# Spectral mixing beside softmax attention: tokens folded four ways instead of two, and the symmetry checks made on chip

## The chip, the core and the metric

One core of a Trainium2 chip runs the whole program. The metric is the device time of one execution in microseconds (us). Its engines are TensorE (PE: matmuls, PEld: its weight loads), VectorE (DVE), ScalarE (ACT), GpSimd (POOL) and SyncE (SP, which here issues all DMAs of the main path).

## The reference

Two branches work on separate inputs, and their outputs stand side by side in `out` (2048 tokens, 2 x 448 features).

```python
# A: Fourier mixing, S = 2048, D = 448
a = einsum("bsd,ed->bse", x, dft_hid_re);  b = einsum("bsd,ed->bse", x, dft_hid_im)
y = einsum("ts,bse->bte", dft_seq_re, a) - einsum("ts,bse->bte", dft_seq_im, b)
# B: softmax attention, 16 heads of 28
q, k, v = split(x @ wqkv);  p = softmax(q @ k.T * 28 ** -0.5);  out = (p @ v) @ wo
```

The DFT matrices are inputs of 2048 x 2048 and 448 x 448. The kernel may use their symmetry only where it finds that the given matrices have it.

## The kernel before

Matmuls run in f32r with each operand split into a high and a low part, so that a product takes three matmuls (high-high, high-low, low-high). The value product of attention is plain f32 and takes two passes.

**Attention.** For each head, 16 key tiles of 128 by 4 query chunks of 512. `first_tiles` makes the scores of the first key tile, which give the row shift: the score matmul (L1107), an ACT copy (L1111), DVE transposes and reductions (L1112, L1113, L1119, L1124), a DVE transpose back (L1133), a cast of the shift into row 96 of q (L1136, POOL or DVE), an addition (L1138, DVE or POOL) and an exponential (L1140). A bank of a first tile is free only after the ACT copy and the DVE transpose. `scores` then has 60 score matmuls a head (L1166), each with an exponential on ACT (L1172); `sums` has the value matmuls in bursts of two key tiles (L1149); `out_of` closes a head (L1198 to L1215). Six of the eight PSUM banks are used for scores and the values' sum, two for everything else. The output projection (L1328) stands behind the last head.

**Fills.** Everything else on PE is put between the scores: the seven q/k projections (L736, L772), the values, and the spectral branch. A planner, `Schedule`, plays the program through once with a table of durations and writes the instructions out, engine by engine, in the order in which it saw them start. Each task has a key; an engine takes the lowest key of those that are ready. `fkey` spreads the keys of the fills over the time up to `T_FILL` in proportion to their planned matmul time, `F_TOTAL`. On the chip each engine, and SP's queue of DMAs, keeps that order.

**Spectral branch.** `hidden` (L888) makes, for the cosine and then the sine part, 8 token tiles of u: tokens s and 2048 - s are added or subtracted (`Pair`, L868), and a tile is multiplied by 226 of the 448 feature columns (`load_folded`, L550); the other columns follow from symmetry at the end. `sequence` (L960) multiplies 8 output tiles by u: for each of two halves it loads a piece of the sequence matrix, splits it (`Piece`, L574: POOL cast L458, POOL subtraction L591) and does 9 matmuls of 452 or 226 columns (L994). The mirrored images of that matrix have to be compared with it before its symmetry may be used. For that, DMAs first write turned copies of both matrices into HBM (`turn_rows`, L854, tensors `wr`); `sequence` reads them back, and `mirrored` (L651) takes differences on POOL or DVE (L654, L672) and their largest values on DVE (L645). The cosine part's result goes through HBM (`y_d`). At the end `flag` puts all checks together; where one fails, general loops (`any_scores`, `any_sequence`) do the work again.

The lines that set the order around the change:

```python
T_ATT, T_END, T_FILL, T_OUT = 56.0, 670.0, 735.0, 690.0
fill_s, bank_s = Slots(banks[:NFILL]), Slots(banks[NFILL:])    # NFILL = 2
M512, M448, M225, MS = 0.2335, 0.2050, 0.1900, 0.2365          # planned us of a matmul
at = 6 + IN + V_PACE * (HEAD - IN)
return at + (f - HEAD) * (T_FILL - at) / (F_TOTAL - HEAD)      # fkey, behind the values
either = {"POOL": 1.2, "DVE": 0.83}                            # planned us of a difference
```

## Time and profile before

| | us |
|---|---|
| runs (median; lowest to highest) | 771.15; 768.4 to 773.13 |
| the profiled execution, first to last instruction | 771.8 |
| PE busy / ACT / DVE / POOL in it | 748.9 / 609.4 / 521.2 / 362.2 |
| end of head 0's values, of head 15's (copies L1198) | 122.0, 733.2 |

The profile comes from one execution, whose span is 0.65 us above the median of the runs; no other time is listed for it. Busy times of PE include the part of a matmul that overlaps the next one.

### The profile page before, as it was taken

Reading aid. Unit: us, or ns where it says so; the run is one execution under the profiler, and the core shown is the slowest. Engines: PE = TensorE matmul, PEld = TensorE weight load, DVE = VectorE, ACT = ScalarE, POOL = GpSimd, SP = SyncE. Lnnn points to the kernel's source line nnn. Section 1 sums busy time; section 2 is a strip of 40 time slices with the busy share of each in tenths; the row PEclk is TensorE's granted clock in tenths of the full one; section 3 lists DMA queues with packets and bytes.
Section 4 is the critical chain, followed back from the end, with each engine's and each line's share of the span. In section 5 each row is a group of like instructions: output and inputs, shape, how many; then the busy total and the mean of one; then the engine's idle time right before and its main releaser. Section 6 shows DMA issues by size and latency. Waiting matters only on the chain.

```text
span 771.8 us, 13016 instructions
## 1 busy us (share of the span) xinstructions
PE 748.9 (97%) x4150; PEld 425.8 (55%) x4150; DVE 521.2 (68%) x962; ACT 609.4 (79%) x1231; POOL 362.2 (47%) x448
## 2 busy tenths in 40 slices
PE   9999999999999999899899999999999989999997
PEld 7899655555555555445455554534545435434596
DVE  5547813656364948899896959695999779834371
ACT  6403888999898988979788989886989869898842
POOL 7211500223032646677674817374787658343510
PEclk9999999999999999999899999999999989999999
DMA  8866845376415635674537657554576585516153
GB/s 309 272 233 186 252 125 159 123 193 199 134 61 146 200 105 164 182 224 135 159 116 221 207 151 230 154 184 131 166 231 215 150 238 158 148 54 209 52 188 137
DMA packets 113603, 133.16 MB, mean 173 GB/s; under 512 B 50345, under 2 KB 63208, under 8 KB 113528
## 3 DMA queue, kind: packets, MB, share of 16 engines
q1 hardware_dynamic: 113528, 132.26, 57.0%
q8 instruction: 35, 0.57, 0.3%
q14 instruction: 40, 0.33, 0.1%
HBM read 101.17 MB, written 49.19 MB: 195 GB/s over the span
## 4 chain that ended last, share of the span: by engine, by line
PE 72%; DVE 9%; DMA 6%; POOL 4%; ACT 4%; issue 3%; SPq 1%; POOLq 0%; ACTq 0%; DVEq 0%
PE bank L1166 24%; PE bank L1149 23%; PE bank L736 12%; PE bank L1328 5%; PE bank L994 4%; ACT kept L1172 3%; PE bank L772 2%; PE bank L908 2%; DMA wraw<-wim 2%; PE bank L1107 1%; DMA wr<-wim 1%; DMA wraw<-wr 1%; DVE kept L1138 1%; DVE mb L1133 1%; DVE mb L1112 1%
## 5 line engine op out<-in xcount | busy, mean ns | idle before, releaser
L1172 ACT ACTIVATE kept<-bank 128x512 f32<-128x512 f32 x960 | 487.0, 657 | 77.6 <-PE bank L1166 77.3
L1166 PE MATMUL bank<-q,k 98*128 98x512 f32 x960 | 341.7, 428 | 6.6 <-ACT kept L1172 4.1
L1166 PEld LDWEIGHTS bank<-q,k 98*128 98x128 f32 x960 | 173.9, 189 | 176.3 <-issue 95.0
L1149 PE MATMUL bank<-kept,v 128*32 128x512 f32 x2048 | 247.8, 608 | 0.0
L1149 PEld LDWEIGHTS bank<-kept,v 128*32 128x32 f32 x2048 | 55.7, 110 | 120.9 <-issue 117.9
L1136 POOL CAST q<-mb 1x512 fp32r<-1x512 f32 x39 | 32.2, 842 | 79.4 <-DVE mb L1133 60.7
L1112 DVE STREAM_TRANSPOSE mb<-bank 128x512 f32<-128x512 f32 x64 | 45.1, 707 | 24.0 <-PE bank L1107 21.9
L1111 ACT ACTIVATE kept<-bank 128x512 f32<-128x512 f32 x64 | 38.4, 651 | 26.0 <-PE bank L1107 21.1
L1209 POOL TENSOR_TENSOR kept<-kept 128x512 f32<-128x512 f32 x16 | 20.7, 1291 | 80.4 <-DVE kept L1204 58.5
L645 DVE TENSOR_REDUCE far<-wraw 128x1 f32<-128x508 f32 (+1 forms) x90 | 57.3, 665 | 0.9 <-POOL wraw L654 0.4
L736 PE MATMUL bank<-big,whi 128*128 128x512 f32 x154 | 57.4, 397 | 0.3 <-DVE wd L753 0.3
L994 PE MATMUL bank<-big,whi 128*128 128x452 f32 x128 | 48.2, 376 | 5.2 <-POOL whi L458 5.2
L591 POOL TENSOR_TENSOR wlo<-wraw,whi 128x512 fp32r<-128x512 f32 (+1 forms) x33 | 43.5, 1319 | 7.9 <-ACT whi L585 5.2
L654 POOL TENSOR_TENSOR wraw<-wraw,wraw 128x508 f32<-128x508 f32 x33 | 37.9, 1149 | 15.2 <-DMA wraw<-wr 6.0
L1140 ACT ACTIVATE kept<-kept 128x512 f32<-128x512 f32 x64 | 41.2, 720 | 4.4 <-DVE kept L1138 3.7
L1133 DVE STREAM_TRANSPOSE mb<-am 128x512 f32<-128x512 f32 x64 | 43.3, 697 | 1.5 <-POOL q L1136 0.5
L1113 DVE TENSOR_REDUCE qm<-mb 128x16 f32<-128x512 f32 x64 | 43.0, 675 | 1.1
L1138 DVE TENSOR_TENSOR kept<-kept,mb 128x512 f32<-128x512 f32 x40 | 38.8, 986 | 0.2
L458 POOL CAST whi<-wraw 128x512 fp32r<-128x512 f32 x30 | 20.0, 665 | 37.1 <-DMA wraw<-wre 13.9
L736 PE MATMUL bank<-wd,big 128*128 128x448 f32 x176 | 37.0, 364 | 0.0
L1200 DVE STREAM_TRANSPOSE kept<-kept 128x512 f32<-128x512 f32 x16 | 11.2, 700 | 37.8 <-ACT kept L1198 37.8
L753 DVE TENSOR_TENSOR kept<-bank,kept 128x512 fp32r<-128x512 f32 x20 | 13.3, 687 | 34.3 <-ACT kept L752 34.2
(165 smaller groups left out, 1017.2 us busy)
## 6 DMA issues: line engine op xcount, KB each, us to landing
wraw<-wr SPq DMA_DIRECT2D x60, 256.0 KB
qkd<-kept SPq DMA_DIRECT2D x40, 256.0 KB
wraw<-xa SPq DMA_DIRECT2D x32, 256.0 KB
wraw<-wre SPq DMA_DIRECT2D x32, 256.0 KB
wr<-wre SPq DMA_DIRECT2D x31, 256.0 KB
wr<-wim SPq DMA_DIRECT2D x31, 256.0 KB
k<-qkd SPq DMA_DIRECT2D x64, 112.0 KB
q<-qkd SPq DMA_DIRECT2D x64, 112.0 KB
```

The source lines that it names most:

```text
L591: b = sch.add(e, at, lambda g: eng[g].tensor_tensor(self.lo.t[:, :n], raw.t[:, :n], f32(self.hi.t)[:, :n], op=ALU.subtract), deps=[a], acq ...
L645: far_done.append(dve(key, lambda: nc.vector.tensor_reduce(far[:, part, n:n + 1], t(), axis=AX.XY, op=ALU.max, apply_absolute_value=True), ...
L736: nc.tensor.matmul(o.t[:, :cols], w(), x(), start=(i == 0), stop=(i == n - 1))
L994: nc.tensor.matmul(o.t[:, :2 * E if slot and slot.pool is whi else E], a, b, start=first, stop=final)
L1112: t = dve(key, lambda o=o, tm=tm: nc.vector.transpose(tm.t, o.t), 0.73, deps=[m], acq=[tm], use=[o], lock=[o], own=RAW_S)
L1113: rs.append(dve(key, lambda tm=tm, c=c: nc.vector.tensor_reduce(qm.t[:, 0, c * NT:(c + 1) * NT], tm.t.rearrange("p (j r) -> p j r", r=32), ...
L1133: t = dve(key, lambda mb=mb, c=c: nc.vector.transpose(mb.t, f32(am.t)[:, c * NT:(c + 1) * NT].unsqueeze(2).to_broadcast([P, NT, 32])), 0.7 ...
L1138: sh = sch.add({"DVE": 0.92, "POOL": POOL_2}, key, lambda e, s=s, mb=mb: eng[e].tensor_tensor(s.t, s.t, mb.t, op=ALU.add), deps=[t, made[c ...
L1140: shown.append(act(key, lambda s=s: nc.scalar.activation(s.t, s.t, AF.Exp, scale=SCALE), ACT_S, deps=[sh], use=[s.pair]))
L1149: nc.tensor.matmul(o.t[c * VW:(c + 1) * VW, :], VT[h].t[:, kt // 4, kt % 4, :], tiles[c].t, start=(kt == 0), stop=(kt == NT - 1))
L1166: m = pe(key, lambda e, o=o, q=q, kt=kt: nc.tensor.matmul(o.t, KT[h][kt // 4].t[:KM, kt % 4 * P:(kt % 4 + 1) * P], q.t[:KM, :], start=True ...
L1172: es[h, kt].append(act(key - 20, lambda o=o, p=p: nc.scalar.activation(p.t, o.t, AF.Exp, scale=SCALE), deps=[m], use=[o, p.pair]))
```

## The change

The spectral branch is written anew.

- **Tokens** s, 2048 - s, 1024 - s and 1024 + s are added and subtracted at once (`tokens`), so that even and odd rows of the sequence matrix, taken apart, need a quarter of it. Features d and 448 - d are folded as well. `features` multiplies the folded tokens (8 fills of 12 matmuls of 226 columns), `sequence` the result (8 fills of 12 or 13).
- Of the sequence matrices only a **base** of 512 x 512 entries each is split and kept on chip (`convert`). All results stay on chip between the two parts.
- The other entries are **compared** with the base in eight `check`s, which only load rows (`Rows`, `Turned`), take differences of up to 1024 columns (L944, POOL or DVE) and their largest values (L887, DVE). The checks' keys are 75, 141, 207 and so on up to 537. No turned copy is written to HBM.
- The planner's durations: 0.107 for a matmul of 226 columns, and 2.3 (POOL) or 1.2 (DVE) for a difference of 1024 columns. `F_TOTAL` is smaller; `T_FILL` and the attention's keys are as before.

The core of the diff:

```diff
-    M512, M448, M225, MS = 0.2335, 0.2050, 0.1900, 0.2365
+    M512, M448, M226, MS = 0.2335, 0.2050, 0.1070, 0.2365
-    F_TOTAL = 7 * F_QKV + F_V + 2 * (NH + 1) * (4 * M448 + 3 * M225) + 2 * NH * (8 * M448 + 9 * M225)
+    F_TOTAL = 7 * F_QKV + F_V + (8 * 12 + 2 * 6 + 8 * 12 + 4 + 2 * 6 + 1) * M226
-    either = {"POOL": 1.2, "DVE": 0.83}
+    either = {"POOL": 2.3, "DVE": 1.2}
+    half_e = {"POOL": 1.25, "DVE": 0.65}
-    wr_d = [dram.tile([NT, P, NH, P], F32, name=f"wr{i}") for i in range(2)]
-    wraw = new("wraw", [P, 4, P], F32, 8, True)
+    raw_s = new("raw", [P, 2, CH], F32, NRAW, True)
...
+    def tokens(c, key, after):
...
+        ts = sch.add(either, key + 1, lambda g: eng[g].tensor_tensor(a.t, n.t, r.t, op=ALU.add), deps=[*ln, *z], use=[n, a, r])
+        td = sch.add(either, key + 1, lambda g: eng[g].tensor_tensor(r.t, n.t, r.t, op=ALU.subtract), deps=[ts], use=[n, r])
...
+    def features(i, ready):
+        for q in range(4):
+            key, o = fkey(12, M226), fill_s.slot()
...
+            end = fill(jobs, key, o, [*x_ready[i], *ready])
...
+    def largest(t, ready, part, key, use, rows=P, d=1.2, n=None):
...
+        far_done.append(dve(key, lambda: nc.vector.tensor_reduce(
+            far[:rows, part, n:n + 1], t(), axis=AX.X, op=ALU.max, apply_absolute_value=True), d, deps=[*ready, far_clear], use=use))
...
+    def check(part, ps, i, key, step):
...
+        def against(x, y, op, at, cols, of=None, deps=()):
+            of = of or cols
+            d = {"POOL": 2.3, "DVE": 1.2} if cols == slice(0, H1) else {"POOL": 1.25, "DVE": 0.65}
+            return sch.add(d, at, lambda g: eng[g].tensor_tensor(x.t[:, cols], x.t[:, cols], y.t[:, of], op=op),
+                           deps=[*x.ld, *y.ld, *deps], use=[x.raw, y.raw])
+
+        def natural(r, at):
+            a, b = Rows(part, r, ps, i, 0, at), Rows(part, r, ps, i, 1, at + 0.4)
+            x = against(b, a, turn, at + 4, slice(0, H1))
+            largest(lambda: b.t, [x], part, at + 5, [b.raw])
+            return a, against(a, a, up, at + 5, high, back, [x])
...
+    def convert(part, n, key, after):
+        r = Rows(part, 0, ps, i, 0, key, 5)
...
-    made = hidden(0, w_first, load_folded(w_first, 0, key - 10, after=[v_last[0], *staged]), x_users)
...
-    sequence(1, made, range(NH - 1), free=[NH - 2])
+    for i in range(2):
+        for c in (2 * i, 2 * i + 1):
+            tokens(c, fkey(0, 0) - 30 + 3 * (c % 2), x_users)
+        features(i, wd_ready)
+    peak = middle(wd_ready)
+    fx_last = last[0]
+    for part in range(2):
+        for n in range(4):
+            convert(part, n, fkey(0, 0) - 18 + 2 * n, [last[0]])
+        special(part, fkey(0, 0) - 14, [fx_last])
+        sequence(part, peak)
+    for n in range(8):
+        check(n // 4, n // 2 % 2, n % 2, CHECK_AT + n * CHECK_STEP, CHECK_STEP / 4)
...
-    sequence(1, made, [NH - 1], True)
```

What that does to the order is shown at three places. In the changed kernel scores are L1221, value matmuls L1204, projections L687 and spectral matmuls L855. First PE in head 0, between two bursts of values, before: eight scores with four projection matmuls (L736) between them.

```order
L1166 MATMUL bank_146<-q_108,k_105 128x512
L1166 MATMUL bank_142<-q_109,k_105 128x512
L1166 MATMUL bank_141<-q_110,k_105 128x512
L1166 MATMUL bank_143<-q_111,k_105 128x512
L1166 MATMUL bank_145<-q_108,k_102 128x512
L736 MATMUL bank_140<-big,whi 128x512
L1166 MATMUL bank_146<-q_109,k_102 128x512
L736 MATMUL bank_140<-big,wlo 128x512
L1166 MATMUL bank_142<-q_110,k_102 128x512
```

And the same group in the changed kernel, up to its burst of values.

```order
L1221 MATMUL bank_126<-q_89,k_86 128x512
L1221 MATMUL bank_123<-q_90,k_86 128x512
L1221 MATMUL bank_122<-q_91,k_86 128x512
L1221 MATMUL bank_125<-q_92,k_86 128x512
L1221 MATMUL bank_127<-q_89,k_83 128x512
L1221 MATMUL bank_126<-q_90,k_83 128x512
L1221 MATMUL bank_123<-q_91,k_83 128x512
L1221 MATMUL bank_122<-q_92,k_83 128x512
L1204 MATMUL bank_124<-kept_107,v_87 32x512 x2
```

The group has no fill any more; four groups in head 0 are of this form. Over the heads 1 to 15 the fills on PE stand like this (counted from the order, up to the last value matmul of each head):

| head | 1 | 2 | 3 | 4 | 5 | 6 | 7 | 8 | 9 | 10 | 11 | 12 | 13 | 14 | 15 |
|---|---|---|---|---|---|---|---|---|---|---|---|---|---|---|---|
| before, 512 columns | 38 | 36 | 34 | | | | | | | | | | | | |
| before, 452 and 448 | | | 1 | 26 | 16 | 23 | 23 | 21 | 16 | 11 | 15 | 18 | 17 | 6 | 17 |
| before, 226 | | | 1 | 20 | 14 | 17 | 20 | 23 | 17 | 14 | 16 | 20 | 20 | 7 | 9 |
| change, 512 columns | 34 | 11 | 36 | 36 | 15 | | | | | | | | | | |
| change, 448 | | | | | | | | | | | | | | | 9 |
| change, 226 | | | | | | | 48 | 8 | 52 | 46 | 56 | 11 | | | |

Second, PE in head 7 of the changed kernel, where the first spectral matmuls stand (`big` is the folded tokens here, `wd` the folded features).

```order
L1221 MATMUL bank_124<-q_95,k_83 128x512
L855 MATMUL bank_121<-wd,big 128x226
L1221 MATMUL bank_125<-q_96,k_83 128x512
L855 MATMUL bank_121<-wd,big 128x226 x3
L1221 MATMUL bank_122<-q_93,k_83 128x512
L855 MATMUL bank_121<-wd,big 128x226 x2
```

In the old kernel such places hold one spectral matmul of 452 or 226 columns after a score; now one to three of 226. Third, DVE between the first tiles of heads 2 and 3, before. (L1200 to L1207 close a head, `wraw` holds raw tokens or matrix pieces, L753 splits a projection.)

```order
L1207 TENSOR_REDUCE ok<-sm_135 128x1
L877 TENSOR_TENSOR wraw_79<-wraw_81,wraw_79 128x4x127
L879 TENSOR_TENSOR wraw_79<-xraw,wraw_79 128x4
L1077 TENSOR_REDUCE ok<-v_107 128x1
L753 TENSOR_TENSOR kept_125<-bank_140,kept_125 128x512
L1112 STREAM_TRANSPOSE mb_133<-bank_146 128x512
L1113 TENSOR_REDUCE qm_136<-mb_133 128x16
```

And there in the changed kernel (L944 and L887 belong to a check, L704 is the old L753).

```order
L944 TENSOR_TENSOR raw_75<-raw_75,raw_73 128x1024
L887 TENSOR_REDUCE far<-raw_72 128x1
L887 TENSOR_REDUCE far<-raw_75 128x1
L887 TENSOR_REDUCE far<-raw_73 128x1
L944 TENSOR_TENSOR raw_71<-raw_71,raw_70 128x1024
L704 TENSOR_TENSOR wd<-bank_121,wd 128x512
L887 TENSOR_REDUCE far<-raw_71 128x1
L887 TENSOR_REDUCE far<-raw_70 128x1
L887 TENSOR_REDUCE far<-raw_74 128x1
L944 TENSOR_TENSOR raw_72<-raw_72,raw_74 128x1024
L704 TENSOR_TENSOR wd<-bank_120,wd 128x512
```

Between the first tiles of these two heads DVE now has 12 reductions and 3 differences of 1024 columns of a check, where a few operations on tokens stood.

682 lines of the change are left out of this document (342 added, 340 removed).

## The prediction

> **What bounds the kernel now.** I read the page's busy times and its chain first, then single stretches by time, because the shares of a whole span mix stages with different limits.
>
> ```profile
> span 771.8 us, 13016 instructions
> PE 748.9 (97%) x4150; PEld 425.8 (55%) x4150; DVE 521.2 (68%) x962; ACT 609.4 (79%) x1231; POOL 362.2 (47%) x448
> ...
> PE 72%; DVE 9%; DMA 6%; POOL 4%; ACT 4%; issue 3%; SPq 1%; POOLq 0%; ACTq 0%; DVEq 0%
> ```
>
> PE looks like the only limit: busy for 97% of the span and 72% of the chain that ended last. If that were all, each matmul removed would shorten the run by its own time. The attention loop says otherwise. One of its groups is two key tiles: 8 score matmuls (L1166) into the 5 banks left to scores, 8 exponentials (L1172), and a burst of value matmuls (L1149). The view by stretches, cut at the starts of four value bursts, gives length, then busy time of PE, PEld, DVE, ACT, POOL, and the granted clock:
>
> ```profile
> 100.60:105.45 4.85, 4.85 (x33) 2.61 (x35) 0.69 (x1) 4.03 (x10) 0.00 (x0) 1.00 0.61 178
> 680.06:685.00 4.94, 4.69 (x25) 1.83 (x24) 3.13 (x4) 4.94 (x12) 4.28 (x4) 1.00 0.14 47
> 685.00:689.93 4.93, 4.68 (x25) 1.84 (x25) 0.00 (x0) 4.93 (x12) 0.00 (x0) 1.00 0.13 37
> 689.93:694.43 4.50, 4.50 (x25) 1.84 (x25) 0.00 (x0) 4.03 (x10) 0.00 (x0) 1.00 0.00 0
> ```
>
> The first group also carries projection matmuls put between the scores ("fills"); the other three carry none. Without fills a group still takes 4.50 us, and 4.93 when ACT has two first-tile activations beside its 8 exponentials (ACT is then busy from end to end). So a group gains at most 0.35 us from losing all its fills: ACT and the way through the banks hold the rest, and PE's 97% is largely filler. The pace per head is in the chain, where 32 value matmuls together mark the end of one head and the start of the next:
>
> ```profile
> 120.03 3.57 PE bank L1149 x32
> 160.24 3.57 PE bank L1149 x32
> 199.79 3.57 PE bank L1149 x32
> ...
> 360.04 3.57 PE bank L1149 x32
> 406.43 3.57 PE bank L1149 x32
> 445.84 3.57 PE bank L1149 x32
> 484.99 3.57 PE bank L1149 x32
> 529.59 3.57 PE bank L1149 x32
> ...
> 656.15 3.57 PE bank L1149 x32
> 694.50 3.57 PE bank L1149 x32
> 702.68 1.91 PE bank L1149 x15
> ...
> 731.19 1.85 PE bank L1149 x16
> ```
>
> Heads 1 to 14 run from 120.03 to 694.50, 574.5 us. Quiet heads take 39.15 to 39.6 us (445.84 to 484.99; 160.24 to 199.79). The head before 694.50, with only 13 fills, takes 38.35. Heads 7 and 10 take 46.39 and 44.60, and the bad ones look like this:
>
> ```profile
> 342.00:386.00 44.00, 41.53 (x223) 21.94 (x225) 39.66 (x73) 36.51 (x75) 31.23 (x42) 0.92 0.47 141
> 428.00:466.00 38.00, 38.00 (x227) 19.38 (x225) 27.58 (x52) 33.69 (x69) 16.78 (x20) 1.00 0.63 177
> 507.00:552.00 45.00, 41.79 (x225) 20.37 (x225) 34.31 (x54) 34.87 (x70) 29.35 (x33) 0.92 0.52 151
> 590.00:637.00 47.00, 41.57 (x224) 19.83 (x222) 37.19 (x64) 36.05 (x72) 31.54 (x36) 0.93 0.63 188
> ```
>
> Each bad stretch has more DVE and POOL work than the quiet one, PE idle for 2.5 to 5.4 us, and a mean clock of 0.92 or 0.93. At 39.4 for thirteen heads and 38.35 for the lightest, heads 1 to 14 would take 550.6, so **stalls cost 23.9 us** of the 574.5.
>
> **The change, step by step.** The sum is against the profiled 771.8 us (first to last instruction), 0.65 above the median of the runs, 771.15.
>
> *Fills.* What one costs PE is its distance to the next start:
>
> ```profile
> 188.17 0.39 PE L736 MATMUL bank<-big,whi 128*128 128x512 f32 x1
> 188.40 0.39 PE L1166 MATMUL bank<-q,k 98*128 98x512 f32 x1
> ...
> 615.66 0.27 PE L994 MATMUL bank<-big,wlo 128*128 128x226 f32 x1
> 615.77 0.40 PE L1166 MATMUL bank<-q,k 98*128 98x512 f32 x1
> 616.01 0.37 PE L994 MATMUL bank<-big,whi 128*128 128x452 f32 x1
> 616.22 0.42 PE L1166 MATMUL bank<-q,k 98*128 98x512 f32 x1
> ...
> L994 PE MATMUL bank<-big,whi 128*128 128x452 f32 x128 | 48.2, 376 | 5.2 <-POOL whi L458 5.2
> ...
> L994 PE MATMUL bank<-big,wlo 128*128 128x226 f32 x128 | 34.8, 272 | 1.4 <-POOL wlo L591 1.3
> ```
>
> That is 0.23 us for 512 columns, 0.21 for 452 and 0.11 for 226 (the groups' 376 and 272 ns include what overlaps the next one). With its smaller groups the old spectral branch has 200 of 452 and 198 of 226, 63.8 us; the new one has 221 of 226, 24 us. These 40 us are not the gain, since a fill stands mostly where PE waits for a bank. What counts is how many heads become light. Per head 1 to 14 the order now gives 34, 11, 36, 36, 15 wide fills, none, then 48, 8, 52, 46, 56, 11 narrow ones, none, none. I price heads 1, 3, 4 at 39.5, heads 9 to 11 (5 to 6 us of fills) at 39.1, heads 2, 5, 7 at 38.6, and 6, 8, 12, 13, 14 at 37.8: 38.35 less two or three of the 0.25 to 0.35 us that fills cost a group. Sum 540.6 against 550.6: **-10.0**. Bounds: +0 if every head kept 39.4, and -20 if a light head came down to 37.1.
>
> *Head 0.* Of 200 projection matmuls before its end 176 are left. Eight go from the start, where PE feeds itself (1.9 us); sixteen go from four groups (4 x 0.35): **-3.3**, at most 24 x 0.23 = 5.6, at least 0 if a load is late instead.
>
> *Head 15* runs from 702.68 to 731.19 in six groups of 4.75 on average; its 17 spectral fills go, and 4.50 each gives **-1.5**. The output projection behind it is the same work: 0.
>
> *The old stalls.* They go with their causes, for instance PE waiting for a converted piece at L458:
>
> ```profile
> 624.68 0.47 PE L994 MATMUL bank<-big,whi 128*128 128x452 f32 x1 [2.37 <-POOL whi L458]
> ```
>
> The turned copies in HBM, the loads behind them and the 16 column tiles of each half go, so **-23.9**, from 0 to -23.9.
>
> *The new stalls.* What is late next is DVE. It makes each head's first tiles, and a first tile's bank stays taken until DVE has transposed it, so a DVE that lags holds up scores at once.
>
> ```profile
> L1112 DVE STREAM_TRANSPOSE mb<-bank 128x512 f32<-128x512 f32 x64 | 45.1, 707 | 24.0 <-PE bank L1107 21.9 <-ACT kept L1111 1.8
> ...
> L645 DVE TENSOR_REDUCE far<-wraw 128x1 f32<-128x508 f32 x60 | 38.8, 662 | 0.8 <-POOL wraw L654 0.4
> L1138 DVE TENSOR_TENSOR kept<-kept,mb 128x512 f32<-128x512 f32 x40 | 38.8, 986 | 0.2
> ...
> L654 POOL TENSOR_TENSOR wraw<-wraw,wraw 128x508 f32<-128x508 f32 x33 | 37.9, 1149 | 15.2 <-DMA wraw<-wr 6.0 <-DMA wraw<-wre 5.5 <-DMA wraw<-wim 3.2
> ...
> L753 DVE TENSOR_TENSOR kept<-bank,kept 128x512 fp32r<-128x512 f32 x20 | 13.3, 687 | 34.3 <-ACT kept L752 34.2
> ```
>
> The new checks use operations of 1024 columns, which no row shows. A reduction of 1024 is bounded by one and by two of 508, 0.66 and 1.32; I take 1.25, near two, as the length is in the columns. A two-operand operation of 1024 is bounded by 0.69 below and 2 x 0.99 above; I take 1.7, near two of L1138, whose operands lie in SBUF as well. Between the first tiles of heads 2 and 3 the new order has 12 reductions (11.4 us), 3 operations of 1024 (5.1), three smaller (2.5) and 4 of L704 (4 x 0.69). The head's own chain is about 16 (the quiet 27.6 of 38 us above, less what I count there as spectral work, an estimate). Sum 37.7 of a 39.5 us head, where before some 25 stood. The same count gives 30 to 35 for most of heads 4 to 11, about 39 around head 8 where tokens are folded, and 16 from head 13 on. Old heads with 34 to 40 us of DVE work lost 5 to 7 us, clock included. I expect two such heads, at 6 each, and 2 us where the first matmul of a fill batch waits for its conversion: **+14**. Bounds: 0, and 24 as before; beyond that lies a rival.
>
> The Trainium skill ("VectorE: DVE Perf Modes", the section on the TRN2 errata) gives (N+151)/0.96 for such an fp32 operation, 1.22 us as an estimate at 1024; for 512 it gives 0.69, as L753 shows and L1138 does not. By it the 19 wide operations on DVE take 9 us less, and the sum would be some 3 us lower.
>
> *SP and DMA.* SP keeps its length, 717 rows for 720, and the copies into HBM go, while loads now come in 512-byte runs. A late q or k load would hold up scores; I take 0, from -2 to +6 (one wait like the DMA ones above).
>
> Sum: 771.8 - 10.0 - 3.3 - 1.5 - 23.9 + 14 = **747**.
>
> **The rivals.**
> *No stall is left* (0 for +14): 733. For it: five late heads have hardly any fills and little DVE work. Against it: DVE at 37 to 39 us in two places. If light heads also reach 37.1, 724.
> *Stalls as before* (24 for 14): 757, to 766 with the q and k loads late as well. For it: 1024-column operations on POOL would be twice 1.15, and what waits for one waits longer.
> *Slower: DVE takes over the pace.* If in each of the eight heads with a check a wide operation took 3.3 us (two of L1138 and a POOL operation to wait for) and the small ones 1.7, DVE would need 44.5 us where the head has 39.5, and PE would idle and be clocked down as in the 0.92 rows: 8 x 6 on 733 is 781. It decides from 42 us of DVE per head on. The old 39.66 of 44 speaks for it, L645 (662 ns, beside busy POOL as well) against.
> *Slower: PE is clocked down in light heads.* A group has 3.7 us of PE work (1.85 value, 8 x 0.23 scores); at half clock 7.5 instead of 4.5, over 35 groups, +105: about 840. The three fill-free groups above at clock 1.00 speak against it. The Trainium skill ("TensorE: Matmul & The Clock Gate", on psum-queue depth-cycling) says that short idles between groups of matmuls that cycle through banks can make the clock fall and rise; by that rule this rival is the forecast, and the trace disagrees with 1.00.
> *The change doesn't do what it says*: if the flag at the end found the folded matrices unequal, the general loops would run behind everything, 512 more matmuls of 448 columns and their loads, far over 1000.
>
> **How the numbers follow.** Forecast (738 to 757) 0.54; no stall (724 to 738) 0.16; stalls as before (757 to 766) 0.20; DVE 0.06; clock 0.03; fallback 0.01. A measurement of this kernel can tell about 1% from no change: 763.4 to 778.9 is "same". Of the stalls-as-before case 0.08 lies there and 0.01 of the DVE case, so faster 0.82, same 0.09, slower 0.09. The range 730 to 766 leaves out half of the no-stall case and the last three, 0.18.
>
> **What would show it.** Starts of 32 value matmuls 37.5 to 38.5 apart in heads 12 to 14, fill-free groups of 4.5 at clock 1.00, ACT busy for over 90% there, PE's share below 97%. Right on the stalls: PE idle and a clock under 1.00 in heads 2, 3 and around 8, none behind head 12. I am wrong if light heads stay at 39.4 (something else than PE and ACT paces a head), if wide DVE operations take over 2.5 us, or if q or k loads head SP's waits.

## The result: 14% slower, 882 us

The changed kernel takes 882.1 us (median of four runs, 880.4 to 883.8), where the kernel before takes 769.8 beside it (four runs): a ratio of 1.144, 95% interval 1.139 to 1.149. The forecast was 747, range 730 to 766, and none of its slower rivals (781, 840, over 1000) is near either. The experiments below find why: many of the new loads and stores are shaped so that only about 2 of the 16 DMA engines carry each of them, and the q, k and v loads of attention stand behind them on the same queue.

The page of the changed kernel, its first lines and the chain that ended last:

```profile
span 882.2 us, 12611 instructions
PE 780.7 (88%) x3971; PEld 406.7 (46%) x3971; DVE 492.1 (56%) x826; ACT 613.9 (70%) x1225; POOL 318.0 (36%) x314
...
PE 49%; DMA 17%; DVE 10%; SPq 10%; ACT 5%; issue 4%; POOL 3%; POOLq 0%; DVEq 0%; ACTq 0%
```

No compute engine has more instructions than before, and DVE and POOL are busy for less time (492 for 521 us, 318 for 362). PE shows 32 us more, though with 179 matmuls fewer; its clock fell in the long heads, as shown below. What has grown in the chain is DMA, from 6% to 17%, and SP's queue, from 1% to 10%. The chain in order of time gives the heads (start of 32 value matmuls, length):

```profile
178.24 5.35 PE bank L1204 x32
223.62 3.57 PE bank L1204 x32
273.67 3.57 PE bank L1204 x32
...
635.21 3.57 PE bank L1204 x32
674.67 3.57 PE bank L1204 x32
728.20 3.57 PE bank L1204 x32
766.18 3.57 PE bank L1204 x32
804.16 3.57 PE bank L1204 x32
...
774.36 1.85 PE bank L1204 x16
778.87 1.85 PE bank L1204 x16
```

The light heads came out as forecast: 37.98 us from 728.20 to 766.18 and again to 804.16 (37.8 was the estimate), with a group of 4.51 from 774.36 to 778.87. Most of the heads with comparisons, tokens and output stores take 44 to 62 us instead: 45.38 and 50.05 in the first three rows, 53.53 from 674.67 to 728.20. The chain is dense with waits for loads there. The waits of DVE and POOL, in total, times and longest:

```profile
POOL raw L944 <- DMA raw<-wre: 60.7, 11, 17.0
DVE ok L1132 <- DMA v<-vd: 47.2, 12, 8.8
DVE raw L944 <- DMA raw<-wre: 30.8, 10, 8.3
DVE raw L807 <- POOL raw L806: 26.6, 3, 10.9
```

Operands of the comparisons (L944), tokens (L807 behind L806) and v (L1132) all arrive late. SP's 904 issues of loads and stores take 577 us, where the 767 of before take 410. (With SP's rows for semaphores that is 597 and 449, the figures in the first expectation below.) The stretch in which one comparison's turned loads end (SP's rows, then the view of the DMA engines from 458 to 462; its first row is their mean busy share in tenths, in 40 slices) shows how:

```profile
453.66 1.27 SPq L904 DMA_DIRECT2D raw<-wim  x2
455.03 5.81 SPq L924 DMA_DIRECT2D raw<-wim  x5
460.94 1.39 SPq L1101 DMA_DIRECT2D k<-qkd  x1
...
DMA  1111111111111111111111111111111111111111
GB/s 46 41 41 41 51 41 41 41 41 51 41 41 41 51 41 41 41 51 41 41 41 51 41 41 41 41 51 41 41 41 51 41 41 41 51 41 41 41 51 41
DMA packets 345, 0.17 MB, mean 43 GB/s; under 512 B 6, under 2 KB 345, under 8 KB 345
q1 hardware_dynamic: 345, 0.17, 14.4%
```

Five turned loads (64 KB each, the fifth a single column) hold SP for 5.81 us. Behind them, for 4 us, 43 GB/s move: 345 packets, or 86 per us, at 14.4% of 16 engines, which is **2.3 engines**. Just before, from 455 to 457, with the last two loads of rows under way and the first turned loads just issued, the same view has these rows:

```profile
DMA packets 929, 0.47 MB, mean 233 GB/s; under 512 B 19, under 2 KB 929, under 8 KB 929
q1 hardware_dynamic: 929, 0.47, 97.2%
```

Pieces of the same 512 B run at 465 per us there, on 15.6 engines. Small pieces are not what is slow. Nor is it their place in memory: a busy engine moves 37 pieces of the turned loads per us and 30 of the rows (86 / 2.3 and 465 / 15.6). The other engines have nothing to do.

Two more records of this trace bear that out. Each load updates a semaphore, a counter on which later instructions wait, as its parts land: 16 times for every load of rows (L904), but only 3 times for each of the 80 turned loads (L924), the 36 turned loads of tokens and weights (L567) and the eight stores of L1065. And the five turned loads above are issued in 0.59, 0.55, 1.54, 1.50 and 1.44 us; the first four land at 459.44, 460.94, 462.45 and 463.94, so 1.5 us apart. From the third on an issue takes as long as one such load takes to land behind the one before it, and the k load can be issued only at 460.94. Counted from the start of their issue, q and k loads land after 2.92 and 3.73 us on average, against 2.49 and 2.78 in the kernel `floor` of experiment 12. So they lose about a microsecond or less behind their issue; the rest of their delay lies ahead of it, where SP is held: in the head from 372.3 to 428.4 it is issuing for 49.7 of the 56.1 us.

### The profile page after: what moved, and what is told of

Read it like the earlier page. It is cut to its first block, busy times and chain, and to the rows that moved or that the text cites. A ratio compares the mean times of both kernels' runs of the same rounds, so it can differ in the third digit from the quotient of the medians.

```text
span 882.2 us, 12611 instructions
## 1 busy us (share of the span) xinstructions
PE 780.7 (88%) x3971; PEld 406.7 (46%) x3971; DVE 492.1 (56%) x826; ACT 613.9 (70%) x1225; POOL 318.0 (36%) x314
## 4 chain that ended last, share of the span: by engine, by line
PE 49%; DMA 17%; DVE 10%; SPq 10%; ACT 5%; issue 4%; POOL 3%; POOLq 0%; DVEq 0%; ACTq 0%
PE bank L1221 18%; PE bank L1204 15%; PE bank L687 8%; ACT kept L1227 4%; PE bank L1377 4%; DMA raw<-wre 4%; DMA raw<-wim 3%; DMA v<-vd 2%; DMA raw<-xa 2%; PE bank L855 2%; SPq L924 2%; PE bank L723 2%; DMA raw<-wd 2%; SPq L904 1%; DVE far L887 1%
## 5 line engine op out<-in xcount | busy, mean ns | idle before, releaser
L1221 PE MATMUL bank<-q,k 98*128 98x512 f32 x960 | 363.3, 455 | 73.0 <-ACT kept L1166 30.9
L1221 PEld LDWEIGHTS bank<-q,k 98*128 98x128 f32 x960 | 181.5, 197 | 278.4 <-issue 103.2
L1204 PE MATMUL bank<-kept,v 128*32 128x512 f32 x2048 | 270.3, 653 | 0.0
L1204 PEld LDWEIGHTS bank<-kept,v 128*32 128x32 f32 x2048 | 58.6, 116 | 134.5 <-issue 127.7
L944 POOL TENSOR_TENSOR raw<-raw,raw 128x1024 f32<-128x1024 f32 (+3 forms) x39 | 69.1, 1774 | 129.1 <-DMA raw<-wre 60.7
L887 DVE TENSOR_REDUCE far<-raw 128x1 f32<-128x1024 f32 (+4 forms) x86 | 77.5, 913 | 40.7 <-POOL raw L944 37.8
L944 POOL TENSOR_TENSOR raw<-raw 128x511 f32<-128x511 f32 x31 | 40.6, 1310 | 70.5 <-DVE raw L944 58.7
L1191 POOL CAST q<-mb 1x512 fp32r<-1x512 f32 x34 | 27.1, 814 | 91.7 <-DVE mb L1188 74.6
L687 PE MATMUL bank<-big,whi 128*128 128x512 f32 x132 | 51.5, 421 | 8.6 <-DVE wd L704 6.5
L944 DVE TENSOR_TENSOR raw<-raw,raw 128x1024 f32<-128x1024 f32 (+3 forms) x25 | 25.9, 1040 | 51.1 <-DMA raw<-wre 30.8
L1193 POOL TENSOR_TENSOR kept<-kept,mb 128x512 f32<-128x512 f32 x34 | 45.8, 1354 | 4.5 <-DVE mb L1188 2.9
L1132 DVE TENSOR_REDUCE ok<-v 128x1 f32<-128x512 f32 x16 | 10.9, 682 | 47.2 <-DMA v<-vd 47.2
L687 PEld LDWEIGHTS bank<-big,whi 128*128 128x128 f32 x132 | 26.6, 202 | 14.7 <-DVE wd L704 7.3
L687 PE MATMUL bank<-wd,big 128*128 128x448 f32 x144 | 33.0, 366 | 0.0
```

Source lines behind the costliest of these rows:

```text
L687: nc.tensor.matmul(o.t[:, :cols], w(), x(), start=(i == 0), stop=(i == n - 1))
L887: far_done.append(dve(key, lambda: nc.vector.tensor_reduce(far[:rows, part, n:n + 1], t(), axis=AX.X, op=ALU.max, apply_absolute_value=Tru ...
L944: return sch.add(d, at, lambda g: eng[g].tensor_tensor(x.t[:, cols], x.t[:, cols], y.t[:, of], op=op), deps=[*x.ld, *y.ld, *deps], use=[x. ...
L1193: sh = sch.add({"DVE": 0.92, "POOL": POOL_2}, key, lambda e, s=s, mb=mb: eng[e].tensor_tensor(s.t, s.t, mb.t, op=ALU.add), deps=[t, made[c ...
L1204: nc.tensor.matmul(o.t[c * VW:(c + 1) * VW, :], VT[h].t[:, kt // 4, kt % 4, :], tiles[c].t, start=(kt == 0), stop=(kt == NT - 1))
L1221: m = pe(key, lambda e, o=o, q=q, kt=kt: nc.tensor.matmul(o.t, KT[h][kt // 4].t[:KM, kt % 4 * P:(kt % 4 + 1) * P], q.t[:KM, :], start=True ...
```

## The experiments

Two theories to begin with. **Q**: SP's queue of loads is what is late; attention's own loads and the operands of the comparisons come behind too much on it. **V**: the comparisons' operations block DVE and POOL, as the prediction feared. T, F, W and E came up on the way and stand in the expectations.

Times are single ones beside the kernel before (768.9 to 771.5 us), unless said otherwise; runs of before lie between 768.0 and 773.3, so a few us between two kernels are not read. The planner orders anew when work is taken out; where every instruction kept its place, this is said.

**1. No comparisons** (`no_checks`)

```
-    for n in range(8):
-        check(n // 4, n // 2 % 2, n % 2, CHECK_AT + n * CHECK_STEP, CHECK_STEP / 4)
```

> The eight comparisons of the two matrices are left out (their loads, differences and maxima); everything else of the changed kernel stays. Theory Q (SP's queue of loads is full: it issued loads for 597 us of the 882, against 449 of 772 before, and some 200 us of that are the comparisons' loads): SP falls under 400 us, q, k and token loads come in time, heads take 38 to 39.5 us and the kernel 725 to 745. Theory V (the comparisons' operations stand in DVE's and POOL's own order and block what is behind them): the same 725 to 745. If it stays above 800, both are wrong and the token loads in 104 small pieces, or the new order of the rest, are the cause.

Here and in loads_only the scale in the flag stayed 0, so the general loops ran behind the work (10204 and 10290 us). Only the part ahead of them is read, from the last output matmuls (L1377, L1375 and L1351 in the three kernels):

```profile
875.21 0.76 PE L1377 MATMUL bank<-wd,whi 128*128 128x448 f32 x3
...
774.10 0.76 PE L1375 MATMUL bank<-wd,whi 128*128 128x448 f32 x3
...
860.73 0.76 PE L1351 MATMUL bank<-wd,whi 128*128 128x448 f32 x3
```

Without the comparisons the work ends 101.1 us sooner, at 774.86. That is not the 725 to 745 of either theory: something else costs 30 to 40 us too.

**2. The comparisons' loads alone** (`loads_only`): `check` only makes its `Rows` and `Turned` tiles.

> The comparisons' loads are all issued as in the changed kernel, but no operation reads them: their 64 differences and 86 maxima on DVE and POOL are left out. Theory Q, if what comes late are the attention's own q, k and v loads behind them on SP: 820 to 880. Theory V, or Q with the late operand blocking DVE and POOL as the way to PE: DVE and POOL have nothing to wait for, 730 to 765, with SP as busy as in the changed kernel.

It ends 14.5 us ahead of the changed kernel, at 861.49: some 868 with the 6.2 behind. One of its heads, then one of tiny_loads (experiment 9), in the view by stretches:

```profile
223.70:277.70 54.00, 45.28 (x234) 23.36 (x230) 16.88 (x31) 36.91 (x74) 8.71 (x9) 0.87 0.72 155
...
197.00:237.20 40.20, 40.20 (x234) 21.39 (x230) 17.13 (x31) 36.41 (x74) 8.70 (x9) 1.00 0.27 80
```

The first head takes 54.00 us with DVE busy for 16.88 and POOL for 8.71. So the busy DVE of the forecast's slower rival does not make the long heads; loads do, with nobody reading them.

**3. Plain shapes for the comparisons' loads** (`plain_shape`, every instruction in its place)

```
-    ap=[[2 * row_n, 64], [tile_n, tiles], [1, P]]
+    ap=[[NH * P, 64], [P, NH], [1, P]]                # rows (not those for conversion)
-    at(base + tt * tile_n, [[P, 2], [-2 * row_n, 64], [1, m]])
+    at((nt + 2 * i + tt) * P * P, [[64 * P, 2], [P, 64], [1, m]])        # turned
```

> The same instructions in the same order on every engine, and the same bytes; only the source of the comparisons' loads is plain: rows of 4 KB that lie together instead of eight pieces of 512 B far apart, and pieces of 512 B in rising order instead of turned ones. What is compared is therefore not the mirrored part, and the flag leaves the comparison out. Theory Q with the shape as the cause: a plain load takes 0.37 us of SP (the median of the x loads) where these take 0.60 to 2.3, so SP loses about 100 of its 597 us, and the kernel takes 770 to 800. Theory Q with the number of issues as the cause: 850 to 885. Theory V: nothing changes on DVE and POOL, 870 to 890.

828.1: 54 us gone with the same number of issues, and the first five long heads back at 40 to 42 us. The shape matters; 780 would have been all of it.

**4. One plain load for each tile** (`plain_loads`): `Rows` and `Turned` issue a single load of 128 rows of 4 KB.

> Each tile of the comparisons is filled by one plain load of 256 KB instead of two loads of pieces (rows) or five to nine (turned rows): 80 issues in place of 208, the same operations on DVE and POOL; what is compared is not the mirrored part, and the flag leaves it out. Theory Q: the comparisons' loads cost SP 80 x 0.4 = 32 us instead of some 200, and the kernel takes 730 to 765. Theory V: the operations are all there, 850 to 885.

831.5, between the theories. SP's rows fall to 432 us, 412 of them issues, and yet the heads from 120.8 on take 47.5, 45.0 and 49.1 us, with DVE and POOL fuller than in plain_shape (35.75 and 30.50 us in the first, 33.90 and 22.02 there):

```profile
120.80:168.30 47.50, 42.49 (x235) 22.61 (x231) 35.75 (x51) 37.26 (x73) 30.50 (x25) 0.96 0.75 249
...
125.70:167.60 41.90, 39.48 (x210) 20.11 (x214) 33.90 (x48) 36.05 (x73) 22.02 (x18) 0.96 0.85 193
```

The planner puts the comparisons closer together here, since it counts fewer loads. The run mixes two causes, and nothing is concluded but that the number of issues is not the main one.

**5. No comparisons, timed** (`no_checks_again`, three rounds)

```
-    nc.vector.tensor_tensor(ok[:, 2 * H:2 * H + 2], f[:, 40:42], f[:, 42:44], op=ALU.is_le)
+    nc.vector.tensor_tensor(ok[:, 2 * H:2 * H + 2], f[:, 40:42], f[:, 40:42], op=ALU.is_le)
```

(The same line takes the comparison out of the flag in the other kernels that load other data.)

> The changed kernel without the eight comparisons (loads, differences, maxima), and with the flag leaving them out, so that the general loops do not run behind the work. The first part of the run before without comparisons ended its last output matmul at 774.9 us, 1.1 us later than 875.97 - 101.1. Theory Q: SP has some 390 us of issues and the kernel takes about 781 (774.9 and the 6.2 us that follow the last matmul of the changed kernel), so the comparisons cost about 100 us, and the rest of the change gains nothing against 771 because the token loads still crowd SP in a few heads. If the time were 735 to 745, the general loops had disturbed the first part.

(The 774.9 is 875.97 less 101.1; the "1.1 us later" in that text means nothing.) 779.4, a ratio to before of 1.011, interval 1.006 to 1.016. **The comparisons cost 103 us**, and without them the change still gains nothing.

**6. Plain token loads as well** (`plain_tokens`): two loads of 256 KB for each of the four chunks in place of 26 small ones.

> As no_checks_again, and the 104 small loads of tokens (rows apart, turned rows, single rows) are 8 plain loads of 256 KB: the spectral branch folds other tokens, with the same operations. Theory Q: what is left of the loss against the forecast (781 against 733, the forecast without new stalls) is the token loads on SP, and the kernel takes 730 to 750. If it stays at 770 to 785, the loss is elsewhere, in the order of the fills or in DVE's and POOL's work.

762.8, so the token loads cost 17 us. The forecast without new stalls, 733, is still 30 away. Two heads stay long, and the chain in them says why:

```profile
380.35 15.54 DMA out<-kept
...
402.79 14.48 DMA out<-kept
```

Exponentials wait for `kept` buffers that the stores of the spectral output still hold. In the changed kernel the same stores give these rows (SP's queue; the chain):

```profile
683.05 7.97 SPq L1072 DMA_DIRECT2D out<-kept  x3
691.13 1.21 SPq L1065 DMA_DIRECT2D out<-kept  x2
692.43 3.10 SPq L1101 DMA_DIRECT2D k<-qkd  x1
...
706.39 11.27 DMA out<-kept
```

**7. The comparisons' loads from POOL** (`pool_queue`, every instruction in its place but on another queue)

```
-    self.ld.append(dma(key, lambda ...: nc.sync.dma_start(...
+    self.ld.append(dma(key, lambda ...: nc.gpsimd.dma_start(...
```

> The whole computation, with the same bytes in the same pieces, but the comparisons' 208 loads are issued by POOL instead of SP. Theory Q with SP's issue time as the limit: SP is free for q, k, v and tokens, and the time falls to 780 to 810, unless POOL needs over 1 us per issue. If the transfers themselves are the limit (512-byte pieces on the DMA engines, busy for 0.6 to 0.8 from 80 to 320 us): 850 to 890, since the bytes and pieces are the same. If POOL's issues cost it several us each: slower still, with POOL late in the trace.

902.0, the slowest run. With the 32 single rows for the tiles' ends, 240 issues move over, and POOL's busy time goes from 318.0 to 482.0 us:

```profile
PE 776.8 (86%) x3971; PEld 407.5 (45%) x3971; DVE 503.4 (56%) x826; ACT 613.8 (68%) x1225; POOL 482.0 (54%) x554
```

POOL stands in each head's first tiles (L1191, L1193), so its lateness is PE's. With 164 us more on POOL, the run doesn't tell what SP's freed time is worth.

**8. True issue costs in the planner** (`real_costs`)

```
-                        at += 0.38
+                        at += issue          # 0.68 rows, 1.15 turned, 0.75 k, 0.7 token pieces, 0.42 else
```

> The whole computation, with the same loads, but the planner that writes the order counts an issue on SP as the trace of the changed kernel shows it (0.68 us for a load of rows, 1.15 for a turned one, 0.75 for k, 0.7 for the token pieces, 0.42 for the others) instead of 0.38 for every one. Theory Q with the order as the fault: the loads that attention waits for go ahead of the comparisons', and the kernel takes 780 to 830. Theory Q with the plain amount as the fault (600 us of issues do not fit): 850 to 890 in any order.

845.1: a better order is worth 37 us, and the transfers stay. SP's rows still add up to 614 us, 577 of them issues.

**9. The same issues, hardly any bytes** (`tiny_loads`, the order of loads_only)

```
-    view()[64 * (1 - b):64 * (2 - b)] ... ap=[[2 * row_n, 64], [tile_n, tiles], [1, P]]
+    view()[64 * (1 - b):64 * (1 - b) + 1] ... ap=[[2 * row_n, 1], [tile_n, tiles], [1, P]]
-    self.t[:, ...] ... [[P, 2], [-2 * row_n, 64], [1, m]]
+    self.t[:2, ...] ... [[P, 2], [1, m]]
```

> As loads_only (no operation reads the comparisons' loads, the same instructions in the same order), but each of the 208 loads brings one or two rows instead of 64 or 128; the flag leaves the comparison out. It parts SP's own issue time from the transfers. Loads_only ended its last output matmul at 861.5 us, 867.7 with the 6.2 behind it; without the loads it is 779. Single-row loads here take SP 0.36 to 0.65 us, so some 100 of the 204 us of issues stay and nearly all bytes go. Theory Q (issue time, whatever the bytes): between the two, 805 to 840. Rival T (the transfers, 33 MB in pieces of 512 B, hold up the other loads): 775 to 790.

788.9, within the rival's range: the **short issues cost 10 us, the bytes 79** (to 868). The issues are not the same in length, though. The comparisons' loads take SP 213 us in loads_only and 122 here (all lines of `Rows` and `Turned`), mostly since the turned ones fall from 1.22 to 0.30 us each. So 122 us of issues cost no more than 10 us, and a count of issues, or a fixed time for each, falls as the cause; the issue time that grows with the transfers is part of the 79. The second stretch under experiment 2 is from this run: 40.20 us, clock 1.00.

**10. Turned loads with rising, adjoining pieces** (`turned_rising`, every instruction in its place): the last line of experiment 3 alone.

> Only the 80 turned loads of the comparisons are changed: the same number of pieces of 512 B, in rising instead of falling order, so what is compared is not the mirrored part and the flag leaves it out; every instruction stays where it was. In plain_shape these loads took SP 0.50 us each where the falling order took 1.14, 51 us less, and the loads of rows 27 us less (106.7 to 87.6 with those for the conversion), for 54 us of time. Theory Q: about two thirds of that, 840 to 855. Theory V or T (pieces of 512 B as such): 870 to 885.

827.5, faster than expected and the same as plain_shape. So all 54 us of experiment 3 belong to the 80 turned loads, none to the rows' 512-byte pieces.

**11. Rising output stores** (`rising_stores`, every instruction in its place)

```
-    t += 2 * (jt * P + 63) + pt
+    t += 2 * jt * P + pt
-    ap=[[P * 2 * D, 2], [-4 * D, 64], [1, D]]
+    ap=[[P * 2 * D, 2], [4 * D, 64], [1, D]]
```

> Only the eight stores of the spectral output that write their rows in falling order are changed to rising order (so these rows of the output stand in another order); all loads and comparisons as in the changed kernel. Head 12 takes 53.6 us there; 11.3 us of its chain are DMA out<-kept, for which an exponential waits, and a k load's issue takes 3.1 us. Theory W (the falling stores are slow and hold kept buffers and the queue): head 12 falls to 39.5 and the kernel to about 868. If the number of stores or v's load is the cause: 880 to 884.

864.0, 18 us less: head 12 falls from 53.6 to 38.1 us. The eight stores were the cause.

**12. All three away** (`floor`): experiments 5, 6 and 11 together.

> No comparisons, plain token loads, and rising stores, so that the spectral output is that of other tokens and in part in another order; the fills, attention and all other work as in the changed kernel. With the stores' part gone (heads 8 and 9 took 50.2 and 42.7 us in plain_tokens, where quiet ones take 38.0): 763 - 16.9 = 746. That would be what the arithmetic of the forecast stands for without new stalls (733). If heads 8 and 9 stay slow: 758 to 765.

746.9, against 746 expected: what the fills are worth once the loads and stores are out of the way, 22 us below the kernel before. That the forecast was 747 as well is chance: 14 us of it were for the comparisons, which this kernel leaves out.

**13. The same rows, rising** (`checks_rising`, every instruction in its place)

```
-    at(base + tt * tile_n, [[P, 2], [-2 * row_n, 64], [1, m]])
+    at(base + tt * tile_n - 126 * row_n, [[P, 2], [2 * row_n, 64], [1, m]])
```

> As turned_rising, with one difference: the 80 turned loads read exactly the same rows, pieces and distances (16 KB apart) as the changed kernel, only from the lowest row up instead of from the highest down; in turned_rising the pieces also lay next to each other. Theory F (a transfer whose rows fall is slow: in the changed kernel, where only such loads are under way, 84 to 86 pieces of 512 B start per us, 43 GB/s, where loads of rows reach 390 to 520 pieces per us): 820 to 835, as turned_rising with 827. If the pieces' lying together was the gain: 865 to 885.

877.2: theory F falls. Rising rows at the same distances are as slow as falling ones (SP's row, then the DMA engines from 456 to 460):

```profile
452.62 5.93 SPq L924 DMA_DIRECT2D raw<-wim  x5
...
DMA packets 345, 0.17 MB, mean 43 GB/s; under 512 B 6, under 2 KB 345, under 8 KB 345
```

**14. All transfers rising** (`all_rising`): experiments 13 and 11, and the token and weight loads (L567) rising.

> All transfers with falling rows are made rising, over the same rows: the 80 of the comparisons, the 36 of tokens and weights and the 8 output stores. Every instruction stays where it was on every engine; the values fold wrongly, and the flag leaves the comparisons out. Theory F: 882 - 55 (as in turned_rising) - 18 (as in rising_stores) - some 25 of the 48 us that four token heads of turned_rising take above 40 us each: 775 to 800. If the token loads' number is their cost, and not the order of their rows: 805 to 812.

865.3, 17 us less than the changed kernel: about what the stores alone gave (18), as F's fall requires. Why the stores gained from it fits what experiment 16 shows: rising, their 2 groups of 64 rows lie at one distance from end to end and make one dimension of 128; falling, they can't. In rising_stores each of the eight stores has 16 semaphore updates instead of 3, and lands 2.2 us after the start of its issue instead of 9.5 (medians). The rising loads keep their 3 updates.

**15. Falling transfers from POOL** (`falling_on_pool`, the whole computation): as experiment 7, but only L924, L567 and L1065.

> The whole computation: only the transfers with falling rows (80 + 36 loads, 8 stores) are issued by POOL, whose descriptors are written by software, where an issue took 0.82 us in pool_queue; SP keeps the rest, nothing else is moved. Theory F: q, k and v no longer stand behind falling transfers, while POOL has 100 us more: 815 to 855. If POOL's place in each head's first tiles decides: 880 to 905, as pool_queue with 902.

854.6, inside F's range, though F is false: these are the same transfers that the next theory names. How much POOL's own order takes back is not shown.

**16. The same rows with the 64 outside** (`checks_wide`, every instruction in its place)

```
-    at(base + tt * tile_n - 126 * row_n, [[P, 2], [2 * row_n, 64], [1, m]])
+    at(base + tt * tile_n - 126 * row_n, [[2 * row_n, 64], [P, 2], [1, m]])
```

> As checks_rising (877: the same rows, pieces and distances as the changed kernel), with one difference: the source of the 80 loads is written as 64 rows outside and 2 pieces inside, not as 2 groups of 64 rows. Theory E (a transfer is dealt out to the DMA engines by its outermost dimension; with 2 there, the packets under way are 2.3 on average and 84 pieces start per us; in turned_rising the two groups lay end to end and made one dimension of 128): 820 to 835, and the pieces of these loads start at several hundred per us. If it is the pieces' lying together in memory: 865 to 885 again.

835.4, 42 us less than checks_rising for two dimensions exchanged. Again SP's row for five loads and the DMA engines, here from 416 to 418:

```profile
414.82 3.17 SPq L924 DMA_DIRECT2D raw<-wim  x5
...
DMA packets 872, 0.43 MB, mean 217 GB/s; under 512 B 57, under 2 KB 871, under 8 KB 871
```

The five issues take 3.17 us in place of 5.93, and 436 packets per us move in place of 86. **Theory E stands**: with 2 entries in the outermost dimension about two engines carry a transfer, with 64 all of them. Each of the 80 loads has 16 semaphore updates here and 3 in checks_rising. In the new order two pieces that lie side by side in memory also follow each other; that is not the gain, since the loads of rows, whose neighbouring pieces lie 1 MB apart, reach 465 pieces per us too. The Trainium skill ("DMA: Bandwidth & Descriptors", section "Rules for kernel authors") has this as a rule: the slowest dimension that isn't 1, of both sides, sets how many engines a transfer is split over, so an outermost dimension of fewer than 16 confines it to at most that many. The 14.4% of 16 engines, the updates and this pair of runs agree with it. Which engines they are, no run here shows.

**17. All of them wide** (`all_wide`, every instruction in its place): experiments 16 and 11, and L567 with `[[row[0], 63], [64 * row[0] - row[1], 2], [1, n]]`.

> As all_rising (865), with the wide order of dimensions for the comparisons' and for the token and weight loads (63 rows outside, 2 inside); the stores are rising, which makes one dimension of 128 of theirs. Every instruction stays in its place. Theory E: 882 - 55 - 18 for comparisons and stores, and less what the token loads lose, 0 to 25: 784 to 809. If E holds for the comparisons alone, about 809.

807.6, against 865.3 for all_rising: 58 us for the order of dimensions in two kinds of loads, 42 of them in the comparisons' (experiment 16 against 13). The 36 loads of L567 have 10 updates each here, 3 in all_rising.

**18. Wide, and nobody reads** (`wide_loads_only`)

> As loads_only (867.7 up to the end of its work), with the wide order of dimensions in the 80 loads: no operation reads the comparisons' loads. It tells what is left of the comparisons when their transfers are spread. If SP's issues are the rest, as tiny_loads has it (789, against 779 without any): 785 to 800, and the operations on DVE and POOL cost what is missing to checks_wide. If bytes and pieces still hold up q and k: 805 to 830, near checks_wide.

814.0, in the second range: bytes and pieces, with the 39 us by which their issues are longer, still cost 25 us above tiny_loads when spread. The operations on DVE and POOL come to 21 (to 835.4), with what the planner's other order changes.

No version here beats the kernel before with the whole computation done. The natural repair, turned rows with 64 outside, needs an outermost dimension that falls; no such transfer was run, and the wide kernels read the rows in another order instead.

## Why the prediction was wrong, step by step

| part | us | from |
|---|---|---|
| fills lighter, most old stalls gone | 746.9 | floor |
| output stores on 2 engines | +16.0 | plain_tokens |
| token loads | +16.6 | no_checks_again |
| comparisons: short issues | +9.5 | tiny_loads |
| comparisons: bytes, spread over all engines, and their longer issues | +25.1 | wide_loads_only |
| comparisons: DVE and POOL operations | +21.4 | checks_wide |
| comparisons: turned loads on 2 engines | +46.7 | the changed kernel, 882.1 |

Each is a difference to the line above, by kernels that leave out a part; the size of one also depends on what else is there (the turned loads are 42 us by experiment 16 against 13, 55 by experiment 10). Three steps keep every instruction in its place: the stores, the spread bytes and the turned loads. In the other three (tokens, short issues, operations) the planner's order changes too, so their sizes are less sure.

- **The step that failed is "SP and DMA: I take 0, from -2 to +6".** It counted rows on SP (717 for 720) and took equal number for equal time. The number was not equal, since such a row can stand for several issues (x5 above): the traces have 904 for 767. Nor was the time, 577 us for 410. What weighs most is that 124 of these transfers ran on about 2 engines, held SP in its next issues and so delayed q, k and v: 114 us of the 135 lost against the forecast stand in the table's lines on stores, tokens and the comparisons' loads, 63 of them in the two lines that only have transfers on 2 engines. (Of the other 21 us, 14 are the floor's 746.9 against the 733 forecast without new stalls, and 7 the term for DVE.) The text named "loads now come in 512-byte runs" as the risk. The length of the pieces was harmless (465 per us); their outermost dimension, `[P, 2]`, stood in the diff.
- **DVE's new stalls, +14**, were about the right size, 21 by experiment 18 (in another order, so not clean), though for bounds of single operations that were partly off. By form:

```profile
L887 DVE TENSOR_REDUCE far<-raw 128x1 f32<-128x1024 f32 x40 | 48.2, 1208 | 15.3 <-POOL raw L944 14.6
...
L944 POOL TENSOR_TENSOR raw<-raw,raw 128x1024 f32<-128x1024 f32 x19 | 46.3, 2437 | 62.8 <-DMA raw<-wre 37.8 <-DMA raw<-wim 13.2 <-DMA qkd<-kept 9.6
...
L944 DVE TENSOR_TENSOR raw<-raw,raw 128x1024 f32<-128x1024 f32 x13 | 16.1, 1237 | 31.7 <-DMA raw<-wre 20.7 <-DMA raw<-wim 9.2 <-issue 1.7
```

  A reduction of 1024 takes 1.21 us (1.25 taken), an operation of two operands 1.24 on DVE (1.7 taken). Here the formula of the Trainium skill ("VectorE: DVE Perf Modes", the section on the TRN2 errata), 1.22 as an estimate, was nearer than the row of L1138. The prediction says that no row shows 1024 columns. The trace of before has some, on one partition: a DVE cast (L691) of 1.22 us and a two-operand operation on POOL (L689) of 2.55, close to the 1.24 and 2.44 measured here.
- **Fills, -10.0, head 0, head 15 and the old stalls, -23.9**: together 733 was forecast without new stalls; the floor's span is 745.3. Light heads are right (37.99 from 437.15 to 475.14 there), and heads 7 to 14 take 306.6 us for 307.1. Heads 1 to 6 still take 39.5 to 41.3 each, 241.4 for 233.5, so either the early heads were priced 8 us too low or some old stalls stay even with plain loads; which, no run here tells. Head 0 ends at 120.0 in no_checks_again and at 120.6 in floor (122.0 before): -1.4 to -2 for the -3.3. Head 15 takes 36.4 us for 36.7 before: -0.3 for the -1.5 (nine matmuls of the output projection stand in it now). What follows it takes 40.2 for 38.7, where no change was forecast. In the changed kernel head 0 ends at 130.3, since comparisons and token loads reach into it.
- **The slower rivals.** DVE as the pace (781) priced the wrong engine: experiment 2 has long heads with DVE at a third of its time. The clock in light heads (840) did not come: the stretches of 4.51 and 37.99 us run at 1.00, so by this trace, too, the Trainium skill's rule on cycling through banks ("TensorE: Matmul & The Clock Gate", on psum-queue depth-cycling) does not bite here. The clock did fall, to 0.77 in one of the long heads of the changed kernel, but that head waits for loads: 21.5% of its chain is DMA raw<-xa, the tokens. The view by stretches, of the changed kernel and, last, of floor:

```profile
372.30:428.40 56.10, 44.41 (x196) 16.84 (x192) 29.84 (x52) 35.11 (x70) 19.43 (x20) 0.82 0.30 80
...
490.60:539.80 49.20, 42.03 (x184) 17.40 (x188) 33.04 (x53) 34.72 (x70) 24.84 (x28) 0.77 0.29 70
...
774.36:778.87 4.51, 4.51 (x28) 1.84 (x32) 1.85 (x3) 4.03 (x9) 0.00 (x0) 1.00 0.29 79
...
437.15:475.14 37.99, 37.49 (x196) 14.87 (x200) 15.08 (x28) 34.52 (x70) 7.07 (x6) 1.00 0.19 50
```

- What would have told it ahead: the text said that it would be wrong "if q or k loads head SP's waits". That sign could not tell, because the line of the q and k loads heads SP's waits in the trace of before too (L1046, 87.5 us behind scores; L1101, 114.3 us, now). A row of before could. It has no turned load in attention, but its eight mirrored copies `out<-yd` (L1037) also have 2 entries in their outermost dimension, `[half, 2]`. They have 3 semaphore updates each and land 7.6 to 9.7 us after the start of their issue, where the stores of 224 KB beside them (L1035) have 16 updates and land after 2.0 to 5.6. So the slowness of such a shape could be read; what it does to q, k and v behind it could not. The range for it should have been wide and on the slow side, and was 8 us.

## What to carry to other kernels

Price a DMA by its shape, not by its row: issue time, and above all the outermost dimension of its source and destination. The same 64 KB in the same 512-byte pieces went at 43 GB/s with 2 groups of 64 rows and at 217 with 64 groups of 2. Such transfers hold the queue's next issues (0.6 us grew to 1.5 above), so ask first what stands behind them; here it was the q, k and v loads that keep PE fed, and matmuls saved on PE counted for little against it. And when a kernel has a single in-order queue, test a suspicion by turning one shape with every instruction in its place: that run is clean where taking work out lets a planner reorder everything.

## What was not expected of the hardware

- Turning rows from falling to rising did nothing for a load (882.1 to 877.2), and 18 us for eight stores, because the rising store is one dimension of 128 (16 semaphore updates) and the falling one is 2 by 64 (3 updates).
- An issue on SP is not of fixed length: turned loads take 1.14 us on average in the changed kernel and 0.66 in checks_wide with the same count, bytes and place. A k load's issue behind the stores took 3.10 us.
- POOL as the issuer cost 164 us of its own busy time for 240 issues, 0.68 us each.
- Open: why the comparisons' 38 MB (128 loads of 256 KB, 64 of 64) still cost 25 us when spread; what part of plain_loads' 831 is order; and how the loss divides between SP's longer issues and later landings, which come together in every pair of runs here.
